# Attention kernel: the gates' matrix set up in the wait for the first keys, the last queries split behind the first maximum, the product's bank copied out by ScalarE

## The chip, the cores and the metric

The kernel runs on one core of a Trainium2 chip. The metric is the device time of one execution in microseconds (us). Engines are named as the profile names them: PE is TensorE's matmul row and PEld its weight load, DVE is VectorE, ACT is ScalarE, POOL is GpSimd, SP is SyncE, which issues nearly all DMAs.

## The reference

Three layers follow each other: attention with rotary positions, a mixture of experts with one expert per token, and a gated layer. The change touches the first one alone.

```
q_rot, k_rot = (rotate(q), rotate(k))          # 4 batches x 8 heads x 576 tokens x 64
scores = scale * q_rot @ k_rot^T
attn = exp(scores - max(scores))
attn = attn / (sum(attn) + 1e-9)
x = attn @ v                                   # tokens x 512
logits = x @ w_gate; expert = argmax(logits)   # 8 experts; a second gate w_output_gate
... experts, then  (sigmoid(x @ w_gate) * (x @ w_val)) @ w_out
```

## The kernel before

**Pairs and steps.** Two heads make a pair g, of which there are 16. A pair has 5 blocks of queries j: four of 128 queries of each head, and one (j = 4) that holds the last 64 queries of both. The text calls 5g + j the step t, from 0 to 79. The order of each engine's work is the order in which the code is written: the loop over t at lines 1042 to 1105 calls the pieces in turn, and every engine works through its own instructions in that order. In a step stand, one after the other:

- `scores(g, j)` (line 262): 12 matmuls (6 for j = 4) of queries and keys, each split in a rounded high part and a rest (`qTh`, `qTl`, `kTh`, `kTl`; `qDh`, `qDl` for the last 64 queries), into two PSUM tiles `s`; then DVE takes the two row maxima `nm` (L285) and ACT the two exponentials `p` (L292). There are two `s` tiles, so the scores of a step can only begin to overwrite them when the exponentials of the step before have read them.
- `pv` of step t - 2 (line 332): the product of weights and values, 18 matmuls (L339, L347) into the one PSUM bank `o` of the pair. After j = 1 and after j = 4 the bank's columns are copied into the SBUF tile `oT` (L349; L351 and L352).
- `turn_last` of step t - 1 (L310 on PE, copy L311 on DVE), then in some steps a piece of `xf`, which turns `oT` back to tokens with the matrix `wI` and divides by the sums, or of `tqk`, which turns the rotated queries and keys of the next pair (L241 and L249 on PE, halves on DVE by L230 and L231).
- `turn` of step t - 1: eight transposes of the weights in two PSUM tiles (L325), each copied by ACT into `pt` (L328). The PSUM tiles `t` come from a ring of three that `turn_last`, `tqk`, `xf` and `turn` share, so the second tile of `turn` needs the one that L311 reads.

POOL rotates the queries and keys two pairs ahead (`rot`, lines 188 to 212).

**The start.** Lines 977 to 995 load the first queries and keys, clear tiles on DVE and POOL, rotate pair 0 on DVE and turn it with `tqk(0, nc.scalar, (30, 8, 0))`: here ACT makes the high halves, and the numbers say how many transposes of the identity stand ahead of the keys, the queries and the tails (the last 64 of both). Their results are never read.

**Late set-up.** `late_setup` after step 2 clears `wI` on POOL and loads constants `mc` and the gates' columns of `wI`. `late_setup2` (line 1020) after step 5 fills `wI` with four identities, makes `tri`, `fold`, `ones`, `ids_tok` and `base` on DVE; `xf`, from step 8 on, and the routing of tokens to experts use them.

**Routing** of a batch (`route`, line 427) is spread over the steps 24 to 34, 44 to 54 and 64 to 74, mostly on DVE.

Of the kernel before, what the change touches and what calls it, by code (L numbers as in the profile page):

```python
# [9 lines left out]
F32 = mybir.dt.float32  # L10
# [5 lines left out]
ALU = mybir.AluOpType  # L16
# [27 lines left out]
XW = DM + 1  # L44
# [21 lines left out]
def tile_kernel(  # L66
# [144 lines left out]

        return a, b

    def tqk(g, eng=nc.vector, spin=(0, 0, 0)):

        i = g % 2

# [25 lines left out]

            return f

        def tails():
            ps = place(2)
            for n, nm in enumerate("kq"):
                nc.tensor.transpose(ps[:, 64 * n : 64 * n + 64], rotd.pop((g, nm))[0:64, 4, :], idf[0:64, 0:64])  # L249
            for c in (0, 576):  # L250
                halves_of(*(t[:, c : c + 64] for t in kT[i]), ps[:, 0:64], "k")
            for e in range(2):
                r = slice(64 * e, 64 * e + 64)
                halves_of(*(t[r, r] for t in qD[i]), ps[r, 64:128], "q")

        return [main("k"), main("q"), tails]

# [74 lines left out]
    def pv(g, j):  # L332
        if j == 0:
            OPS[g] = po.tile([128, 512], F32, tag="o", name="o")
        ps, src, (va, vd) = OPS[g], PT.pop((g, j)), vraw[g]
        q0, n = (128 * j, 128) if j < 4 else (0, 64)
        for c in range(4):
            for e in range(2):
                nc.tensor.matmul(  # L339
                    ps[64 * e : 64 * e + 64, q0 : q0 + n],  # L340
                    va[:, e, c, :],
                    src[:, 4 * e + c, :] if j < 4 else src[:, c, 64 * e : 64 * e + 64],
                    start=(c == 0),
                    stop=False,
                    skip_group_check=True,
                )
        nc.tensor.matmul(ps[:, q0 : q0 + n], vd, src[:, 8, 0:n], start=False, stop=True, skip_group_check=True)  # L347
        if j == 1:
            nc.vector.tensor_copy(O[g % 2][:, 0:256], ps[:, 0:256])  # L349
        elif j == 4:  # L350
            nc.vector.tensor_copy(O[g % 2][:, 256:512], ps[:, 256:512])  # L351
            nc.vector.tensor_copy(O[g % 2][:, 512:576], ps[:, 0:64])  # L352

# [628 lines left out]
        nc.vector.memset(t, 1.0)  # L984
    for t in (*(x.bitcast(F32) for x in (*qD[0], *qD[1])), *(vd for _, vd in vring + vlast)):
        nc.vector.memset(t, 0.0)
    load(1)
    load(0, "v")
    R = {nm: rot(0, nm) for nm in "kq"}
    for nm in "kq":  # L990
        for f in R[nm]:
            f(eng=nc.vector)
    first, gate_q = tqk(0, nc.scalar, (30, 8, 0)), rotd[0, "q"]
    for f in first:
        f()

    nc.gpsimd.tensor_copy(scr, gate_q[0:1, 0, 0:1])
    load(2)
# [4 lines left out]

    def late_setup():
        nc.sync.dma_start(out=mc, in_=misc)
        nc.gpsimd.memset(wI, 0.0)
        nc.gpsimd.memset(pinit, DUMMY)
        for t in O:
            nc.gpsimd.memset(t[:, 576:640], 0.0)
        nc.sync.dma_start(out=x_dram[0:1, :], in_=wI.rearrange("p h w -> p (h w)")[0:1, 0:XW])  # L1010
        for e in range(2):
            r = slice(64 * e, 64 * e + 64)
            for o, w in ((0, w_gate), (E, w_og)):
# [4 lines left out]
                )  # L1018

    def late_setup2():  # L1020
        nc.vector.tensor_copy(wI[:, :, 0:128], idf.unsqueeze(1).to_broadcast([128, 4, 128]))
        nc.vector.tensor_copy(tri, mc[:, 0:128])
        for o in range(2):
            nc.vector.tensor_tensor(
                out=fold[:, 64 * o : 64 * o + 64], in0=idf[:, 0:64], in1=idf[:, 64:128], op=ALU.add
            )
        nc.vector.memset(ones, 1.0)
        nc.vector.tensor_copy(ids_tok, mc[:, 128:148])
        nc.vector.tensor_copy(base, mc[:, 272:280])
        nc.sync.dma_start(out=perm_dram.rearrange("(p a) o -> p (a o)", p=128), in_=pinit)  # L1030

    M["seq"] = MAIN
# [9 lines left out]
    for t in range(NJ * NPAIR):  # L1042
        g, j = divmod(t, NJ)
        if t == NJ * (NPAIR - 1):
# [6 lines left out]
            gather(0)  # L1051
            gather(1)
        scores(g, j)
        if t >= 2:
            pv(*divmod(t - 2, NJ))
        if t >= 1:
# [316 lines left out]
```

## Time and profile before

| | us |
|---|---|
| median of 3 runs | 1128.62 |
| lowest, highest | 1127.61, 1129.76 |
| the profiled execution | 1129.55 |
| its span | 1127.8 |

The span goes from the first to the last instruction of the program in the profiled execution; 1.75 us lie around it. The attention fills the first 340 us or so of it. PE is the busiest engine, 95% of the span, DVE 68%, ACT 52%, POOL 32%. TensorE's clock has two levels, 2.4 GHz (1.00 in the profile) and 1.2 GHz (0.50); its mean share is 0.986.

### The profile page before, as it was taken

To read this page: it belongs to the slowest core of one execution; us is meant where nothing else is said; L and a number is where in the kernel's file an instruction comes from. 1 tells how busy PE (TensorE), PEld (TensorE's weight loads), DVE (VectorE), ACT (ScalarE), POOL (GpSimd) and SP (SyncE) were. 2 spreads that over 40 slices of the span, in tenths; PEclk is the share of its full clock that TensorE was granted. 3 is DMA by queue.
4 is the path that set the end of the run, shared out by engine and by line. 5 is a ranking of instruction groups with operands and counts; after the bars stand their busy time and mean duration, and the time that the engine had idled before them with its cause. 6 is when DMAs were issued, how large, how long until landed. Compare 5 with 4: busy or idle time off the path is not lost. (4 is left out here: it accounts for less than half of the span.)

```text
span 1127.8 us, 20456 instructions
## 1 busy us (share of the span) xinstructions
PE 1076.3 (95%) x7682; PEld 961.7 (85%) x7682; DVE 771.9 (68%) x1439; ACT 582.2 (52%) x1122; POOL 360.3 (32%) x336
## 2 busy tenths in 40 slices
PE   7799998989998999999999999999999999999998
PEld 6688787778777988988888889888999999999997
DVE  6778787787876886889989868854444545444442
ACT  4466455555544344667667656654444444444432
POOL 6335454553612103444333134521111111111111
PEclk8899999999999999999999999999999999999999
DMA  4144045045008297699999543300010010100000
GB/s 112 37 84 77 12 50 102 9 56 87 30 14 227 48 146 267 197 330 301 324 302 318 200 142 122 103 1 28 1 57 1 10 47 1 57 1 1 28 1 28
DMA packets 97053, 111.61 MB, mean 99 GB/s; under 512 B 16817, under 2 KB 75441, under 8 KB 96946
## 3 DMA queue, kind: packets, MB, share of 16 engines
q1 hardware_dynamic: 92482, 97.81, 31.2%
q0 software_dynamic: 4320, 12.08, 3.7%
q8 instruction: 62, 1.02, 0.4%
q14 instruction: 45, 0.37, 0.1%
q10 hardware_dynamic: 144, 0.33, 0.1%
HBM read 103.03 MB, written 15.56 MB: 105 GB/s over the span
## 5 line engine op out<-in xcount | busy, mean ns | idle before, releaser
L1242 POOL TENSOR_TENSOR gl<-gf,gh 128x384 fp32r<-128x384 f32 x72 | 73.3, 1018 | 348.6 <-ACT gh L1241 348.6
L292 ACT ACTIVATE p<-s,nm 128x576 f32<-128x576 f32 x144 | 105.6, 738 | 125.8 <-DVE nm L285 121.4
L771 DVE TENSOR_TENSOR lo<-wr,hi 128x1024 fp32r<-128x1024 f32 x112 | 156.4, 1409 | 14.7 <-ACT hi L770 14.3
L1237 DVE TENSOR_TENSOR gf<-v,sg 128x384 f32<-128x384 f32 x72 | 40.0, 555 | 134.0 <-PE v L1233 134.0
L285 DVE TENSOR_REDUCE nm<-s 128x1 f32<-128x576 f32 x144 | 102.9, 751 | 39.2 <-PE s L279 26.0
L1241 ACT CAST gh<-gf 128x384 fp32r<-128x384 f32 x72 | 36.9, 513 | 160.5 <-DVE gf L1237 160.5
L1216 DVE TENSOR_TENSOR gl<-gw,gh 128x512 fp32r<-128x512 f32 x72 | 72.9, 1012 | 66.8 <-ACT gh L1215 66.7
L770 ACT CAST hi<-wr 128x1024 fp32r<-128x1024 f32 x106 | 109.7, 1052 | 5.4 <-PE y L861 2.7
L325 PE MATMUL t<-idf,p 128*128 128x128 f32 x576 | 84.4, 282 | 19.0 <-DVE pt L311 16.7
L1231 PE MATMUL t<-yh,gh 128*128 128x384 f32 x288 | 99.1, 344 | 1.8 <-ACT gh L1215 1.6
L1233 PE MATMUL t<-yh,gl 128*128 128x384 f32 x288 | 97.4, 338 | 0.6 <-DVE gl L1216 0.2
L1232 PE MATMUL t<-yl,gh 128*128 128x384 f32 x288 | 96.7, 336 | 0.0
L1233 PE MATMUL v<-yh,vl 128*128 128x384 f32 x288 | 96.2, 334 | 0.0
L1231 PE MATMUL v<-yh,vh 128*128 128x384 f32 x288 | 96.2, 334 | 0.0
L1232 PE MATMUL v<-yl,vh 128*128 128x384 f32 x288 | 96.2, 334 | 0.0
L328 ACT COPY pt<-t 128x512 f32<-128x512 f32 x144 | 79.2, 589 | 31.3 <-PE t L325 30.7
L325 PEld LDWEIGHTS t<-idf,p 128*128 128x128 f32 x576 | 67.1, 146 | 27.1 <-DVE pt L311 21.3
L830 PE MATMUL h<-xl,hi 128*128 128x256 f32 x288 | 82.0, 285 | 1.8 <-DVE sc L806 1.8
L830 PE MATMUL h<-xh,hi 128*128 128x256 f32 x288 | 81.9, 284 | 0.7 <-DVE hl L835 0.7
L830 PE MATMUL h<-xh,lo 128*128 128x256 f32 x288 | 81.5, 283 | 0.0
L1235 ACT ACTIVATE sg<-t 128x384 f32<-128x384 f32 x72 | 35.3, 491 | 81.8 <-PE t L1233 81.8
L861 PE MATMUL y<-hi,hl 128*128 128x512 f32 x184 | 73.0, 397 | 4.6 <-DVE hl L847 4.4
(235 smaller groups left out, 2974.8 us busy)
## 6 DMA issues: line engine op xcount, KB each, us to landing
wr<-in_moe_w_dram SPq DMA_DIRECT2D x112, 512.0 KB
cv<-in_moe_w_gate_dram SPq DMA_DIRECT2D x12, 512.0 KB
cv<-in_moe_w_val_dram SPq DMA_DIRECT2D x12, 512.0 KB
cv<-in_moe_w_out_dram SPq DMA_DIRECT2D x12, 512.0 KB
yt<-y_dram SPq DMA_DIRECT2D x18, 256.0 KB
out_dram<-ob SPq DMA_DIRECT2D x18, 256.0 KB
kraw<-in_k_dram SPq DMA_DIRECT2D x16, 256.0 KB
qraw<-in_q_dram SPq DMA_DIRECT2D x16, 256.0 KB
```

Of the source, the lines that this page charges most:

```text
L285: nc.vector.tensor_reduce(out=nm, in_=s[:, :, 0:288], axis=AX.XY, op=ALU.max, negate=True)
L292: nc.scalar.activation(out=P[g, j][:, e, :].rearrange("p (a b) -> p a b", a=2), in_=s[:, :, 0:288], func=AF.Exp, bias=nm, scale=1.0, accum ...
L325: nc.tensor.transpose(ps[:, 128 * c : 128 * c + 128], src[:, e, k0 + 128 * c : k0 + 128 * c + 128], idf)
L328: nc.scalar.copy(dst[:, 4 * e : 4 * e + 4, :].rearrange("p c q -> p (c q)"), ps)
L770: nc.scalar.copy(out=hi, in_=t)
L771: nc.vector.tensor_tensor(out=lo, in0=t, in1=hi.bitcast(F32), op=ALU.subtract)
L830: nc.tensor.matmul(ps[:, c, :], w[:, kk, 128 * c : 128 * c + 128], x[:, kk, :], start=first, stop=last)
L861: nc.tensor.matmul(ps, hl, rh, start=False, stop=False)
L1231: nc.tensor.matmul(ps[:, 0:TG], wh[:, c], yh[:, kk, :], start=(kk == 0), stop=False)
L1232: nc.tensor.matmul(ps[:, 0:TG], wh[:, c], yl[:, kk, :], start=False, stop=False)
L1233: nc.tensor.matmul(ps[:, 0:TG], wl[:, c], yh[:, kk, :], start=False, stop=(kk == KD - 1))
L1242: nc.gpsimd.tensor_tensor(out=gl, in0=gf, in1=gh.bitcast(F32), op=ALU.subtract)
```

## The change

The memset of `wI`'s last columns, its four identities and `fold` now stand on DVE ahead of the rotation of pair 0. The tails of pair 0 are two pieces: the keys' is turned and halved between the keys and the queries, the queries' after the scores of step 0, behind 14 transposes of the identity; ahead of the queries stand 6 of these instead of 8. `tri`, `ids_tok` and `base` are copied by ACT after step 5, `ones` is set by POOL. The row of zeros in `x_dram` is written from `pinit` in 27 pieces instead of from `wI`. The three copies out of `o` are ACT's.

```diff
-    def tqk(g, eng=nc.vector, spin=(0, 0, 0)):
+    def tqk(g, eng=nc.vector, spin=(0, 0, 0, 0)):
...
-        def tails():
-            ps = place(2)
+        def tails(which="kq"):
+            ps = place(2 if "k" in which else 3)
             for n, nm in enumerate("kq"):
+                if nm not in which:
+                    continue
                 nc.tensor.transpose(ps[:, 64 * n : 64 * n + 64], rotd.pop((g, nm))[0:64, 4, :], idf[0:64, 0:64])
-            for c in (0, 576):
-                halves_of(*(t[:, c : c + 64] for t in kT[i]), ps[:, 0:64], "k")
-            for e in range(2):
-                r = slice(64 * e, 64 * e + 64)
-                halves_of(*(t[r, r] for t in qD[i]), ps[r, 64:128], "q")
+            if "k" in which:
+                for c in (0, 576):
+                    halves_of(*(t[:, c : c + 64] for t in kT[i]), ps[:, 0:64], "k")
+            if "q" in which:
+                for e in range(2):
+                    r = slice(64 * e, 64 * e + 64)
+                    halves_of(*(t[r, r] for t in qD[i]), ps[r, 64:128], "q")
...
         if j == 1:
-            nc.vector.tensor_copy(O[g % 2][:, 0:256], ps[:, 0:256])
+            nc.scalar.copy(O[g % 2][:, 0:256], ps[:, 0:256])
         elif j == 4:
-            nc.vector.tensor_copy(O[g % 2][:, 256:512], ps[:, 256:512])
-            nc.vector.tensor_copy(O[g % 2][:, 512:576], ps[:, 0:64])
+            nc.scalar.copy(O[g % 2][:, 256:512], ps[:, 256:512])
+            nc.scalar.copy(O[g % 2][:, 512:576], ps[:, 0:64])
...
+    nc.vector.memset(wI[:, :, 128:160], 0.0)
+    nc.vector.tensor_copy(wI[:, :, 0:128], idf.unsqueeze(1).to_broadcast([128, 4, 128]))
+    for o in range(2):
+        nc.vector.tensor_tensor(out=fold[:, 64 * o : 64 * o + 64], in0=idf[:, 0:64], in1=idf[:, 64:128], op=ALU.add)
     load(1)
     load(0, "v")
...
-    first, gate_q = tqk(0, nc.scalar, (30, 8, 0)), rotd[0, "q"]
-    for f in first:
-        f()
+    first, gate_q = tqk(0, nc.scalar, (30, 6, 0, 14)), rotd[0, "q"]
+    first[0]()
+    first[2]("k")
+    first[1]()
...
-        nc.gpsimd.memset(wI, 0.0)
...
-        nc.sync.dma_start(out=x_dram[0:1, :], in_=wI.rearrange("p h w -> p (h w)")[0:1, 0:XW])
+        nc.sync.dma_start(out=x_dram[0:1, :].rearrange("o (p c) -> (o p) c", p=27), in_=pinit[0:27, 0:19].bitcast(F32))
...
     def late_setup2():
-        nc.vector.tensor_copy(wI[:, :, 0:128], idf.unsqueeze(1).to_broadcast([128, 4, 128]))
-        nc.vector.tensor_copy(tri, mc[:, 0:128])
-        for o in range(2):
-            nc.vector.tensor_tensor(
-                out=fold[:, 64 * o : 64 * o + 64], in0=idf[:, 0:64], in1=idf[:, 64:128], op=ALU.add
-            )
-        nc.vector.memset(ones, 1.0)
-        nc.vector.tensor_copy(ids_tok, mc[:, 128:148])
-        nc.vector.tensor_copy(base, mc[:, 272:280])
+        nc.gpsimd.memset(ones, 1.0)
+        for o, c in ((tri, slice(0, 128)), (ids_tok, slice(128, 148)), (base, slice(272, 280))):
+            nc.scalar.copy(out=o, in_=mc[:, c])
...
         scores(g, j)
+        if t == 0:
+            first[2]("q")
```

What this does to the order of the engines is shown at three places. The numbers behind tile names tell buffers apart; `x2` stands for two in a row.

DVE at the start, from the rotation of pair 0's queries (`trq`) to the first maxima, before:

```order
L208 TENSOR_TENSOR trq<-ta,tb 128x2x5x64
L231 SCALAR_TENSOR_TENSOR kTl_150<-t,kTh_149 128x512
L231 SCALAR_TENSOR_TENSOR qTl_142<-t,qTh_141 128x512
L231 SCALAR_TENSOR_TENSOR kTl_150<-t,kTh_149 128x64 x2
L231 SCALAR_TENSOR_TENSOR qDl_146<-t,qDh_145 64x64 x2
L285 TENSOR_REDUCE nm<-s 128x1 x4
```

and now:

```order
L208 TENSOR_TENSOR trq<-ta,tb 128x2x5x64
L231 SCALAR_TENSOR_TENSOR kTl_150<-t,kTh_149 128x512
L231 SCALAR_TENSOR_TENSOR kTl_150<-t,kTh_149 128x64 x2
L231 SCALAR_TENSOR_TENSOR qTl_142<-t,qTh_141 128x512
L289 TENSOR_REDUCE nm<-s 128x1 x2
L231 SCALAR_TENSOR_TENSOR qDl_146<-t,qDh_145 64x64 x2
```

The keys' tails moved ahead of the queries, the queries' tails behind the first two maxima.

DVE from the first block of step 6 on, behind the keys of pair 2 (`kTl_150`), before:

```order
L231 SCALAR_TENSOR_TENSOR kTl_150<-t,kTh_149 128x512
L1021 COPY wI<-idf 128x4x128
L1022 CAST tri<-mc 128x128
L1024 TENSOR_TENSOR fold<-idf 128x64 x2
L1027 MEMSET ones 128x128
L1028 CAST ids_tok<-mc 128x20
L1029 COPY base<-mc 128x8
L285 TENSOR_REDUCE nm<-s 128x1 x2
L351 COPY oT_154<-o 128x256
L352 COPY oT_154<-o 128x64
L311 COPY pt<-t 128x128
```

and now:

```order
L231 SCALAR_TENSOR_TENSOR kTl_150<-t,kTh_149 128x512
L289 TENSOR_REDUCE nm<-s 128x1 x2
L315 COPY pt<-t 128x128
L230 TENSOR_SCALAR qTh_141<-t 128x512
L231 SCALAR_TENSOR_TENSOR qTl_142<-t,qTh_141 128x512
```

Between the keys and the maxima nothing is left, and none of the copies of `oT` ahead of L311 (now L315).

ACT at the same place, from the exponentials of step 5 to the copies `pt` of step 5, before:

```order
L292 ACTIVATE p,lsum_156<-s,nm 128x576 x2
L328 COPY pt<-t 128x512
L292 ACTIVATE p,lsum_156<-s,nm 128x576 x2
L328 COPY pt<-t 128x512 x2
L292 ACTIVATE p,lsum_156<-s,nm 128x576 x2
```

and now:

```order
L296 ACTIVATE p,lsum_156<-s,nm 128x576 x2
L332 COPY pt<-t 128x512
L1031 CAST tri<-mc 128x128
L1031 CAST ids_tok<-mc 128x20
L1031 COPY base<-mc 128x8
L296 ACTIVATE p,lsum_156<-s,nm 128x576 x2
L355 COPY oT_154<-o 128x256
L356 COPY oT_154<-o 128x64
L332 COPY pt<-t 128x512 x2
```

The three constants stand ahead of step 6's exponentials, the two copies of `oT` between these and the copies `pt`.

## Rows read from the trace of the kernel before

**Rows 1.** The page: busy time of the engines, share of the span, instructions.

```profile
PE 1076.3 (95%) x7682; PEld 961.7 (85%) x7682; DVE 771.9 (68%) x1439; ACT 582.2 (52%) x1122; POOL 360.3 (32%) x336
```

**Rows 2.** Timeline, steps 5 to 7: start, duration, engine, line, tiles, [idle before <-releaser].

```profile
36.51 1.48 DVE L1021 COPY wI<-idf 128x512 f32<-128x512 f32 x1
...
38.70 2.38 DVE L1024 TENSOR_TENSOR fold<-idf 128x64 f32<-128x64 f32 x2
...
41.83 1.41 DVE L285 TENSOR_REDUCE nm<-s 128x1 f32<-128x576 f32 x2
...
43.96 1.12 PE L325 MATMUL t<-idf,p 128*128 128x128 f32 x4 [5.92 <-DVE pt L311]
```

**Rows 3.** Windows: stretch, length, PE, PEld, DVE, ACT, POOL busy (instructions), PEclk, DMA, GB/s.

```profile
2.54:5.08 2.54, 2.54 (x13) 2.54 (x14) 0.01 (x1) 0.00 (x0) 0.00 (x0) 1.00 0.90 297
13.08:19.91 6.83, 4.45 (x23) 3.52 (x21) 3.37 (x7) 3.16 (x9) 6.67 (x7) 0.50 0.34 90
34.98:49.79 14.81, 8.89 (x86) 7.24 (x85) 12.62 (x25) 5.03 (x12) 9.47 (x8) 0.77 0.09 26
61.53:69.21 7.68, 7.47 (x86) 6.10 (x85) 6.92 (x17) 4.99 (x12) 2.24 (x2) 1.00 0.70 115
```

**Rows 4.** Timeline of DVE at the start.

```profile
5.08 0.82 DVE L193 TENSOR_TENSOR ta<-kraw,ropes 128x640 f32<-128x640 f32 x1 [2.54 <-DMA kraw<-in_k_dram]
```

**Rows 5.** Timeline of DVE at the start of the experts.

```profile
348.93 0.70 DVE L768 CAST hi<-wr 128x1024 fp32r<-128x1024 f32 x1 [2.47 <-DMA wr<-in_moe_w_dram]
```

**Rows 6.** Timeline, steps 0 and 1.

```profile
11.20 0.22 ACT L228 ACTIVATE kTh<-t 128x64 fp32r<-128x64 f32 x1
...
12.84 0.30 PE L279 MATMUL s<-kTl,qTh 64*128 64x288 f32 x2
...
13.72 1.42 DVE L285 TENSOR_REDUCE nm<-s 128x1 f32<-128x576 f32 x2
...
15.25 0.73 ACT L292 ACTIVATE p<-s,nm 128x576 f32<-128x576 f32 x1
...
15.40 1.32 PE L279 MATMUL s<-kTh,qTh 64*128 64x288 f32 x2 [2.27 <-ACT p L292]
...
17.73 1.42 DVE L285 TENSOR_REDUCE nm<-s 128x1 f32<-128x576 f32 x2 [2.58 <-PE s L279]
```

**Rows 7.** Windows of PE alone, in the identity's 30 transposes: busy (instructions), PEclk.

```profile
2.38:4.00 1.62, 1.62 (x8) 1.00 0.86 303
...
7.00:8.00 1.00, 1.00 (x10) 1.00 0.85 208
```

**Rows 8.** Timeline, step 16 (pair 3, block 1) and the start of step 17.

```profile
83.41 0.42 DVE L351 COPY oT<-o 128x256 f32<-128x256 f32 x1
...
83.65 0.73 ACT L292 ACTIVATE p<-s,nm 128x576 f32<-128x576 f32 x1
...
83.87 0.28 DVE L311 COPY pt<-t 128x128 f32<-128x128 f32 x1
...
84.20 0.42 PEld L325 LDWEIGHTS t<-idf,p 128*128 128x128 f32 x4 [0.44 <-DVE pt L311]
...
84.37 1.12 ACT L328 COPY pt<-t 128x512 f32<-128x512 f32 x2
84.79 0.19 PEld L279 LDWEIGHTS s<-kTh,qTh 64*128 64x128 f32 x2 [0.17 <-issue]
...
85.78 0.85 PEld L339 LDWEIGHTS o<-pt,v 128*64 128x64 f32 x16 [0.16 <-issue]
...
85.89 0.76 DVE L285 TENSOR_REDUCE nm<-s 128x1 f32<-128x576 f32 x1 [0.41 <-PE s L279]
```

**Rows 9.** Timeline, step 13 (block 3): ACT's copies of the weights.

```profile
73.17 1.07 ACT L328 COPY pt<-t 128x512 f32<-128x512 f32 x2 [0.46 <-PE t L325]
```

**Rows 10.** Loads of weights in routing, steps 26 and 27.

```profile
127.93 0.42 PEld L325 LDWEIGHTS t<-idf,p 128*128 128x128 f32 x4 [0.61 <-DVE pt L311]
```

**Rows 11.** Timeline, a long DVE instruction at step 54.

```profile
246.44 3.69 DVE L535 SCALAR_TENSOR_TENSOR den<-zs,den 128x5 f32<-128x5 f32 x1
```

## The prediction

> **What bounds the kernel now.** I read the page first: PE is busy 95% of the span, the others have room [rows 1]. So only what makes PE wait, or run at its lower clock, can be worth much, and I went through the attention step by step in the timeline for that. Three places concern this change. In step 6 PE stands 5.92 us for the copy L311, because DVE, which works in order, has the whole late set-up ahead of the maxima on which everything of that step hangs [rows 2]. At the start PE works through steps 0 and 1 with waits, and the granted clock is 0.50 (1.2 GHz) from 13.08 to 19.91 [rows 3, 6]. And in each pair's block 1 PE's weight loads wait 0.44 us for L311 behind the two copies of `oT` [rows 8]. Elsewhere the steps follow each other with PE full: the two steps 61.53 to 69.21 hold 7.47 us of PE work in 7.68 [rows 3].
>
> **Term 1, the late set-up leaves step 6.** From the scores of step 6 to those of step 8 pass 14.81 us; the same two steps one pair later, with the same 86 matmul records, take 7.68 [rows 3]. The difference, 7.13 us, is all that the set-up costs: DVE's block from 36.51 to 41.83, which is 5.32 us, and 1.8 us of work at the lower clock that followed the idle time (0.77 in the mean, against 1.00). What is late next is DVE's work on the keys of pair 2: it was free for the set-up at 36.51 [rows 2], 1.53 after the start of the scores at 34.98, while in step 17 the maxima start 85.89 - 84.79 = 1.10 after it [rows 8]. So 0.43 stays: a gain of 7.13 - 0.43 = 6.70 us.
>
> Where did the work go? ACT's three small copies, each between the 0.22 of 64 columns and half the 1.12 of two times 512 [rows 6, 8], come to between 0.7 and 1.7 us; at 128, 20 and 8 columns I take 0.7. They lie in front of step 6's exponentials, in the time in which ACT waits for the first maximum of the step, in every step; it has only the one copy `pt` of block 4 to do there. Without that cover they would delay the exponentials one for one. POOL's `ones` stands between rotations that are needed two pairs later, and POOL is rid of the memset of `wI`; nothing waits. SP's row of zeros waits for `pinit` instead of `wI`, both on POOL and in that order of lines; the loads behind it are used from step 8 on. All at nothing.
>
> **Term 2, the set-up in the wait for the first keys.** DVE is idle for 2.54 us up to the landing of the keys at 5.08 [rows 4]. Into it go a memset of 128 columns, a copy of 512 and two sums of 64. Their bounds: 1.48 + 2.38 us, as copy and sums took in step 5 beside a busy POOL [rows 2], which with the memset would end some 1.5 us after the keys and delay everything by that; or the row of a 1024-column cast on DVE, 0.70 [rows 5], for no more columns than all four have together (128 + 512 + 128 = 768), with some 0.1 for each further instruction about 1.0. POOL does nothing in this stretch, 0.00 [rows 3], so I take the lower value: hidden, with 1.5 us to spare.
>
> **Term 3, the split tails.** Before, the last scores of step 0 end at 13.14 but the maxima start only at 13.72, since the four tails in turn on ACT and DVE stand ahead [rows 6]. Now the keys' tails stand ahead of the queries' halves. ACT's second tail follows DVE's first, which is behind `kTl`; I expect it at 10.97, so that the queries' high half starts some 0.25 later than now, and the scores end at about 13.4 instead of 13.14. The maxima follow at once: 0.28 earlier than 13.72. The exponentials then end at 15.70 instead of 15.98. The queries' tails come behind them on ACT and are done on DVE by about 16.7, ahead of the next maxima: free as long as the scores of step 1 end later than that.
>
> The 14 transposes of the identity fill PE's 2.27 us of waiting [rows 6]. If they keep the clock up, the scores of step 1, which took from 15.40 to 17.92 at 1.2 GHz, take about 1.05 as in later steps and end at 16.85; their maxima, at 17.73 now, come 0.85 us earlier, and this carries through. But the clock fell at 13.08, before PE's long wait had begun, and the change takes activity away ahead of it, not adds any. If it falls all the same, the 14 take 0.20 us each, as the first 8 of the 30 did in 1.62 us, and not the 0.10 of the later ones [rows 7]: 2.9 us, to 16.6, which is later than the exponentials. Then the scores of step 1 end at 17.9 if the clock is back by then, no gain, or at 19.1 if it is not: 1.3 us lost. Between -0.85 and +1.3 I take 0.
>
> A rule speaks against these transposes. The Trainium skill, page "TensorE: Matmul & The Clock Gate", section "Part 4: PE-mode transpose", says that the full clock does not engage for transposes, as they do not count as PE activity in the same way. By that they would cost the 1.3 us and hold nothing. This trace disagrees in part: 30 transposes alone stood ahead when their pace went from 0.20 to 0.10 us each [rows 7].
>
> **Term 4, the copies out of the bank.** DVE is rid of three copies in each pair, ACT has them. In block 1 before, L311 started at 83.87 behind the two copies; now it starts where they did, at 83.41, and the 0.44 us wait goes. But the next wait stands right behind: the scores of step 17 need the second exponential, which ends at 83.65 + 0.73 = 84.38, so they start at 84.45 instead of 84.79, 0.34 earlier [rows 8]. And ACT now does both copies after that exponential: by the 0.22 of 64 columns and the 1.07 of two times 512 [rows 6, 9], some 0.37 and 0.22, less about 0.1 overlap each, 0.40. `pt` is then done at about 84.37 + 0.40 + 1.08 = 85.85 instead of 84.37 + 1.12 = 85.49, and the product that needs it starts at 85.92 instead of 85.78 [rows 8]. The gain of 0.34 becomes a loss of 0.14. In block 3 ACT waits 0.46 us for PE ahead of `pt` [rows 9], and the 256 columns fit in. Where routing makes DVE late, its shorter queue does help: the 0.61 us wait of step 27 [rows 10] shrinks by about 0.45; the three routings have some four such places, and about two where ACT has no slack in block 3 and 0.3 is lost. Sum: ten usual pairs at +0.14, four at -0.45, two at +0.3, that is +1.4 - 1.8 + 0.6 = +0.2. The bounds: -0.34 in 14 pairs, -4.8, and +0.3 in 14, +4.2, if ACT's copies cost 0.16 more than I think. I take 0.
>
> **Sum.** 6.70 us off the profiled execution's 1129.55 gives 1122.85; the median of the runs is 0.93 below that execution, so 1121.9.
>
> **The rivals.**
> - ScalarE keeps up, and block 1 gains its 0.34 in all 14 pairs: 1121.9 - 4.8 = 1117.1. For it: `pt` was done 0.29 ahead of the product [rows 8]. Against: the copies take more than that.
> - ACT's copies cost 0.3 in each pair: 1121.9 + 4.2 = 1126.1. For it: nothing but ACT's order decides; against: the two durations above.
> - The slower side: ScalarE becomes the bound of the attention. If each copy costs ACT the 0.42 that the wide one cost DVE [rows 8], without overlap, and a wait of its own besides, block 1 loses and block 3 eats its 0.46. The kernel is slower than before by more than 0.2% from 0.64 us a pair ((6.70 + 2.26) / 14); at 0.8 it is 1121.9 + 11.2 = 1133. Against: ACT's rows of 64 and 512 columns.
> - A pause goes or comes. DVE stood 3.69 us in one tiny instruction at step 54 [rows 11], and a second such pause stands in the trace; with the clock that falls after it, as after the 5.92 us in term 1 (1.8), each costs some 5 us. The change moves DVE's instructions against the loads. One gone: 1117; one more: 1127.
> - The 14 transposes hold nothing (the skill's rule above): 1121.9 + 1.3 = 1123.2.
> - The set-up isn't hidden at the start: 1121.9 + 1.5 = 1123.4, folded into the forecast's spread.
>
> **Chances.** Forecast, 1120 to 1124: 0.52. ScalarE keeps up: 0.15. Copies cost 0.3: 0.12. A pause gone 0.08, one more 0.05. Transposes hold nothing: 0.05. Slower: 0.03. A measurement of this kernel can tell 0.2%, 2.26 us, from no change, so faster means below 1126.36. That holds for the forecast, the first rival, a pause gone, the transposes, and rather more than half of the second: 0.87. Within 0.2%: the rest of it and one more pause, 0.10. Slower: 0.03. The range 1116.5 to 1126.0 leaves out one more pause, the slower side and part of the second rival, some 0.15.
>
> **What would show it.** Right: maxima of step 6 at about 36.6 of the new span, no wait over 0.5 us in steps 5 to 8 and clock 1.00 there; DVE's `fold` done ahead of the keys; L315's wait gone in block 1 and a new wait of PE for `pt` ahead of the product. Wrong: steps of pair 0 longer than 4.6 us, `fold` over 1 us each at the start, block 1 shorter than 3.8 us to the product, or DVE standing 3 us and more at other places.

## The result and the profile after

The changed kernel takes 1118.39 us, median of 4 runs (1117.05 to 1119.51), beside 1128.57 (1127.61 to 1129.76) of the kernel before on the same chip: 10.2 us less, a ratio of 0.990 (95% interval 0.9879 to 0.9921). A second set of 6 runs on another chip gave 1117.31 beside 1126.07: 0.9921 (0.9901 to 0.9940). The forecast was 1121.9 in 1116.5 to 1126.0: faster, as said, but by half as much again as the 6.7 us of the sum.

The profiled execution after took 1117.64 us, its span 1115.9 (before 1129.55 and 1127.8). The page's first part, beside [rows 1]: VectorE lost 18 us of busy time, ScalarE gained 10, TensorE has the same work in less time.

```profile
PE 1076.5 (96%) x7694; PEld 962.6 (86%) x7694; DVE 753.9 (68%) x1388; ACT 592.2 (53%) x1173; POOL 360.4 (32%) x336
```

Windows of after (stretch, length, busy time and instructions of PE, PEld, DVE, ACT, POOL, PEclk, DMA share, GB/s): from the first scores to those of step 5; the two steps from step 6 to step 8; the same two of the next pair.

```profile
11.88:30.80 18.92, 17.48 (x171) 14.53 (x171) 12.15 (x25) 10.91 (x28) 17.76 (x19) 1.00 0.20 46
34.31:42.08 7.77, 7.77 (x87) 6.46 (x86) 6.48 (x15) 5.72 (x17) 6.53 (x8) 1.00 0.18 50
53.81:61.57 7.76, 7.76 (x86) 6.45 (x86) 6.47 (x15) 5.32 (x14) 1.96 (x2) 1.00 0.70 116
```

The second row is the answer to the 14.81 us of [rows 3]: PE is busy all the time, at clock 1.00, and the steps are as long as the next pair's. The third shows that a usual pair gained nothing (7.76 now, 7.68 before).

**Where the time went**, stage by stage. Each number is the time between the first scores matmuls of two steps in the trace of one execution; the last column is the changed kernel on the second chip.

| steps | before | after | difference | after, again |
|---|---|---|---|---|
| start to 5 | 31.46 | 30.80 | -0.66 | 31.71 |
| 5 to 8 | 18.32 | 11.28 | -7.04 | 11.28 |
| 8 to 25 | 66.46 | 66.71 | +0.25 | 66.71 |
| 25 to 30 (first routing) | 22.96 | 21.93 | -1.03 | 21.93 |
| 30 to 64 | 147.03 | 146.26 | -0.8 | 144.9 |
| 64 to 79 (third routing, slots) | 66.98 | 64.16 | -2.8 | 64.31 |
| 79 to the end | 774.57 | 774.74 | +0.2 | 773.9 |

The differences add up to 11.9 us, by which these two executions differ; the medians differ by 10.2. Steps 5 to 30 agree in the two executions of the changed kernel to 0.1 us. Steps 30 to 64, the start and the end do not, to some 1 us. Within 30 to 64 lies the second routing: steps 45 to 50 took 23.00 us before, 22.18 and 21.97 after.

### The profile page after: what moved, and what is told of

The parts are those of the page before. It is cut to its first block, busy times and chain, and to the rows that moved or that the text cites. A ratio compares the mean times of both kernels' runs of the same rounds, so it can differ in the third digit from the quotient of the medians.

```text
span 1115.9 us, 20490 instructions
## 1 busy us (share of the span) xinstructions
PE 1076.5 (96%) x7694; PEld 962.6 (86%) x7694; DVE 753.9 (68%) x1388; ACT 592.2 (53%) x1173; POOL 360.4 (32%) x336
## 5 line engine op out<-in xcount | busy, mean ns | idle before, releaser
L775 DVE TENSOR_TENSOR lo<-wr,hi 128x1024 fp32r<-128x1024 f32 x112 | 156.2, 1408 | 14.9 <-ACT hi L774 14.6
L1220 DVE TENSOR_TENSOR gl<-gw,gh 128x512 fp32r<-128x512 f32 x72 | 72.9, 1012 | 66.9 <-ACT gh L1219 66.8
L329 PE MATMUL t<-idf,p 128*128 128x128 f32 x576 | 81.3, 280 | 6.0 <-DVE pt L315 3.7
L1260 PE MATMUL o<-oh,gl 128*128 128x512 f32 x192 | 76.3, 397 | 0.1
```

The costliest lines, as they stand in the source:

```text
L329: nc.tensor.transpose(ps[:, 128 * c : 128 * c + 128], src[:, e, k0 + 128 * c : k0 + 128 * c + 128], idf)
L775: nc.vector.tensor_tensor(out=lo, in0=t, in1=hi.bitcast(F32), op=ALU.subtract)
L1260: nc.tensor.matmul(ps, gl[:, c], wh, start=False, stop=(f == NF - 1))
```

## The experiments

Fourteen traces (before, after and one of each run below) carry what follows; every time was taken beside the kernel before on the same chip, so kernels of different chips are compared by their ratio to it. A single median here has an interval of some 2 us to either side. Up to step 30 the traces of kernels whose code in a stretch is the same agree to 0.2 us, so differences of stretches decide where medians can't. Later stretches spread more: steps 64 to 79 took 66.98, 65.14 and 65.46 us in before and experiments 2 and 3, whose code there is the same.

### 1. The late set-up back in step 5

```diff
-    nc.vector.memset(wI[:, :, 128:160], 0.0)
-    nc.vector.tensor_copy(wI[:, :, 0:128], idf.unsqueeze(1).to_broadcast([128, 4, 128]))
-    for o in range(2):
...
     def late_setup2():
-        nc.gpsimd.memset(ones, 1.0)
...
-            nc.scalar.copy(out=o, in_=mc[:, c])
+        nc.vector.tensor_copy(wI[:, :, 0:128], idf.unsqueeze(1).to_broadcast([128, 4, 128]))
+        nc.vector.tensor_copy(tri, mc[:, 0:128])
+        for o in range(2):
...
+        nc.vector.tensor_copy(base, mc[:, 272:280])
```

> The changed kernel with the late set-up alone back as it was: on VectorE behind the maxima of step 5, the memset of wI on GpSimd; start, split tails and copies out of the bank as changed. Theory (the set-up cost 7.1 us of waiting in steps 5 to 7 and nothing at the start): 6.7 to 7.1 us above the changed kernel, about 1125.3, with the wait of step 6 back and the times of steps 0 to 4 unchanged to 0.1 us. Rival (most of what was won came from elsewhere, the set-up at the start costs something too): under 5 us above the changed kernel, and steps 0 to 4 earlier by 0.2 us or more.

Measured: 1119.89, ratio 0.9937 (0.9914 to 0.9959), 2 to 4 us above the changed kernel by the ratios. Steps 5 to 10 take 22.94 us beside 19.50: only 3.44 more. That is between the 6.7 to 7.1 of the theory and nothing, and steps 0 to 4 came no earlier, though the rival wanted that. The same instructions, in the same place, were done in 2.3 us, where they had taken 5.3. VectorE and GpSimd in that stretch (start, duration, engine, line, operation, tiles, [idle before <-releaser]):

```profile
36.45 0.42 DVE L1026 COPY wI<-idf 128x512 f32<-128x512 f32 x1
36.79 0.22 DVE L1027 CAST tri<-mc 128x128 bf16<-128x128 f32 x1
36.92 0.36 DVE L1029 TENSOR_TENSOR fold<-idf 128x64 f32<-128x64 f32 x2
37.25 0.17 DVE L1032 MEMSET ones<- 128x128 bf16 x1
37.33 1.43 DVE L1033 CAST ids_tok<-mc 128x20 int32<-128x20 f32 x1
...
38.75 1.41 DVE L289 TENSOR_REDUCE nm<-s 128x1 f32<-128x576 f32 x2
```

```profile
37.19 1.54 POOL L193 TENSOR_TENSOR ta<-kraw,ropes 128x640 f32<-128x640 f32 x1 [6.89 <-DMA kraw<-in_k_dram]
38.69 1.67 POOL L200 TENSOR_TENSOR tb<-kraw,ropes 128x320 f32<-128x320 f32 x2
```

The copy of `wI` took 0.42 here and 1.48 in [rows 2], the two sums of `fold` 0.36 against 2.38. GpSimd was still idle. The first instruction with an input that met it, a cast of 20 columns issued at 37.33, ended at 38.76, 0.03 after GpSimd's L193. In the kernel before, GpSimd had begun a little earlier:

```profile
36.16 1.55 POOL L193 TENSOR_TENSOR ta<-kraw,ropes 128x640 f32<-128x640 f32 x1 [6.20 <-DMA kraw<-in_k_dram]
37.66 1.85 POOL L200 TENSOR_TENSOR tb<-kraw,ropes 128x320 f32<-128x320 f32 x2
39.47 1.53 POOL L193 TENSOR_TENSOR ta<-qraw,ropes 128x640 f32<-128x640 f32 x1
```

There the copy of `wI` ended at 37.99, 0.28 after the first L193, and the two sums of `fold` at 39.59 and 41.08, each 0.08 after a GpSimd instruction (39.51 and 41.00).

New theory: VectorE's instructions on tiles in SBUF stand until GpSimd's running one has ended, and this, not their work, was most of what the set-up cost.

### 2. The kernel before, its set-up one step earlier

```diff
-        if t == 5:
+        if t == 4:
             late_setup2()
```

> The kernel before, with its late set-up on VectorE called one step earlier, behind the tails of step 4, where GpSimd does nothing; nothing else is changed. Theory (VectorE's instructions on tiles in SBUF stand still until GpSimd's running instruction ends, so the set-up took 5.32 us beside GpSimd's rotation and would take 1.4 to 1.6 without it): step 5's maxima 1.2 to 1.6 us later, steps 6 and 7 back to about 3.5 and 4, the kernel 4.5 to 5.5 us faster than before, about 1121.5. Rival (the set-up's own work and its place on VectorE cost the 7 us): the wait of some 5 us is then found in step 5, the kernel within 1 us of before.

Measured: 1120.04, ratio 0.9946 (0.9926 to 0.9966), 6.0 us faster than before by this one number. VectorE has the same instructions, now with GpSimd idle until 37.26:

```profile
33.12 0.43 DVE L1021 COPY wI<-idf 128x512 f32<-128x512 f32 x1
33.46 0.22 DVE L1022 CAST tri<-mc 128x128 bf16<-128x128 f32 x1
33.60 0.35 DVE L1024 TENSOR_TENSOR fold<-idf 128x64 f32<-128x64 f32 x2
33.93 0.17 DVE L1027 MEMSET ones<- 128x128 bf16 x1
34.01 0.11 DVE L1028 CAST ids_tok<-mc 128x20 int32<-128x20 f32 x1
34.03 0.15 DVE L1029 COPY base<-mc 128x8 f32<-128x8 f32 x1
34.22 1.42 DVE L285 TENSOR_REDUCE nm<-s 128x1 f32<-128x576 f32 x2
```

1.06 us in place of 5.32. Steps 4 to 8 take 15.75 us (22.13 before): 6.4 us of the 7 are had without moving the set-up off VectorE's path at all. The theory holds.

### 3. The kernel before with the move of the set-up alone

Against the kernel before, and with the row of zeros taken from `pinit`, as changed:

```diff
+    nc.vector.memset(wI[:, :, 128:160], 0.0)
+    nc.vector.tensor_copy(wI[:, :, 0:128], idf.unsqueeze(1).to_broadcast([128, 4, 128]))
+    for o in range(2):
...
     def late_setup2():
-        nc.vector.tensor_copy(wI[:, :, 0:128], idf.unsqueeze(1).to_broadcast([128, 4, 128]))
...
+        nc.gpsimd.memset(ones, 1.0)
...
+            nc.scalar.copy(out=o, in_=mc[:, c])
```

> The kernel before with the move of the set-up alone (early on VectorE, three copies on ScalarE, ones on GpSimd); start, tails and copies out of the bank as before. Theory: 6.7 to 7.1 us faster than before, about 1119.5 to 1121, all of it in steps 5 to 7; usual pairs 19.4, routing steps as before. Rival (the parts help each other: the late maxima of step 6 cost so much only because VectorE met GpSimd there): 3 to 4 us faster.

Measured: 1120.48, ratio 0.9955 (0.9929 to 0.9981). Steps 5 to 8 take 11.19 us, 7.13 less than before; and the ratio's interval, 2 to 8 us of 1126, holds both that and the 5.6 of the medians. In the stretch itself the rival's 3 to 4 us are out. Steps 25 to 30 stay at 23.0. Steps 64 to 79 took 65.46, 1.5 less than before; experiment 4, with the same move and VectorE's copies too, has 66.80, so that difference is the spread of these steps and not the move.

### 4. The three copies back on VectorE

```diff
-            nc.scalar.copy(O[g % 2][:, 0:256], ps[:, 0:256])
+            nc.vector.tensor_copy(O[g % 2][:, 0:256], ps[:, 0:256])
...
-            nc.scalar.copy(O[g % 2][:, 256:512], ps[:, 256:512])
-            nc.scalar.copy(O[g % 2][:, 512:576], ps[:, 0:64])
+            nc.vector.tensor_copy(O[g % 2][:, 256:512], ps[:, 256:512])
+            nc.vector.tensor_copy(O[g % 2][:, 512:576], ps[:, 0:64])
```

> The changed kernel with the three copies of oT back on VectorE. Theory (the copies bring about 0.4 to 0.5 us at each of the routing steps that wait for a ring tile behind VectorE, and more in the third routing and the work on slots, and cost 0.1 in a usual pair): 2.5 to 4 us above the changed kernel, with steps 27, 29 and 65 to 75 longer by what they had lost, and the usual pairs' steps shorter by 0.1 us a pair. Rival (as predicted, the copies come to nothing and the rest is chance in where pauses fall): within 1 us of the changed kernel.

Measured: 1121.52 (12 runs), ratio 0.9955 (0.9936 to 0.9974), 4 to 6 us above the changed kernel by the ratios. Usual pairs 19.40 (19.49 as changed), steps 25 to 30 23.11 (21.93), 64 to 79 66.8 (64.2). So the copies are worth 1.2 us in the first routing and cost 0.1 in a usual pair, as the theory said. In steps 64 to 79 they are worth 2.6 by this trace, and 1 to 3 by the four traces that have them on VectorE (before, experiments 2, 3 and 4: 65.1 to 67.0). The waits of the weight loads of the transposes for VectorE's copy L315, from 38 to 340 us of the span (total us, times, longest), first with the copies back, then as changed:

```profile
PEld t L329 <- DVE pt L315: 11.6, 15, 2.0
```

```profile
PEld t L329 <- DVE pt L315: 3.9, 6, 1.6
```

### 5. Block 1's copy on ScalarE, block 4's on VectorE

```diff
         elif j == 4:
-            nc.scalar.copy(O[g % 2][:, 256:512], ps[:, 256:512])
-            nc.scalar.copy(O[g % 2][:, 512:576], ps[:, 0:64])
+            nc.vector.tensor_copy(O[g % 2][:, 256:512], ps[:, 256:512])
+            nc.vector.tensor_copy(O[g % 2][:, 512:576], ps[:, 0:64])
```

> The changed kernel with block 4's two copies on VectorE where they were, ahead of the copy pt; block 1's copy stays on ScalarE. Tells which copies cost the usual pairs 0.1 us and which bring the gain of the routing steps. Theory (block 4's copies trade a wait for L315 against one for ScalarE's pt, block 1's are free): usual pairs 19.40, step 26 again 4.3, steps 28 and 70 to 75 as in the changed kernel, 5.09 and 21.6. Rival (block 1's copy costs or brings nothing): all steps as with the three copies back, 5.62 in step 28 and 22.55 in 70 to 75.

Measured: 1120.28, ratio 0.9930 (0.9917 to 0.9943). Usual pairs 19.40, step 26 4.31 (3.86 as changed), step 28 5.29 (5.09 as changed, 5.62 with all copies back). So block 4's copies cost the 0.1 in usual pairs and bring the 0.45 in step 26; block 1's bring 0.33 of step 28, the rest is block 4's. Steps 70 to 75 took 24.09, where the theory had 21.6 and the rival 22.55; neither explains that.

### 6. Block 4's copies on VectorE behind L315

```diff
         elif j == 4:
-            nc.scalar.copy(O[g % 2][:, 256:512], ps[:, 256:512])
-            nc.scalar.copy(O[g % 2][:, 512:576], ps[:, 0:64])
+            def out():
+                nc.vector.tensor_copy(O[g % 2][:, 256:512], ps[:, 256:512])
+                nc.vector.tensor_copy(O[g % 2][:, 512:576], ps[:, 0:64])
...
+                late.append(out)
...
             turn_last(*divmod(t - 1, NJ))
+        while late:
+            late.pop()()
```

> The changed kernel with the two copies of block 4 on VectorE again, but behind the copy pt on which the next weight loads wait; block 1's copy stays on ScalarE. Theory (the weight loads of block 1 wait for ScalarE's pt or for the copy L315, whichever has the oT copies ahead of it; behind both they cost nothing): the usual pairs' five steps 19.0 to 19.15 us in place of 19.49, 3 to 4 us faster than the changed kernel over ten pairs, less up to 0.5 in each routing. Rival (the next wait stands right behind, at the transposed block or the exponentials): 19.3 to 19.5, within 1 us of the changed kernel.

Measured: usual pairs 19.13, 0.36 below the changed kernel and 0.27 below before, as the theory said. But 1118.13, ratio 0.9929 (0.9911 to 0.9947), is no gain: steps 25 to 30 take 22.65 (21.93), 30 to 35 20.61 (19.84 and 19.96). Probably the copies are in the way of what stands behind them in VectorE's late steps; which wait it is was not read. From step 5 to 79 it was still faster (308.03 us; 310.33 and 309.12 as changed), and lost that behind step 79 (776.5; 774.7 and 773.9), for a reason that isn't known.

### 7. Behind L315 in usual pairs, on ScalarE where routing follows

Against experiment 6:

```diff
+            cp = nc.scalar.copy if g in (4, 5, 8, 9, 12, 13, 15) else nc.vector.tensor_copy
...
-                nc.vector.tensor_copy(O[g % 2][:, 256:512], ps[:, 256:512])
-                nc.vector.tensor_copy(O[g % 2][:, 512:576], ps[:, 0:64])
+                cp(O[g % 2][:, 256:512], ps[:, 256:512])
+                cp(O[g % 2][:, 512:576], ps[:, 0:64])
...
-            if g < NPAIR - 1:
-                late.append(out)
+            if g in (4, 5, 8, 9, 12, 13, 15):
+                out()
```

> The changed kernel with block 4's copies of oT on VectorE behind the copy pt in the nine pairs 0 to 3, 6, 7, 10, 11 and 14, and on ScalarE as changed in the others, whose products end in routing steps. Theory (0.36 us a usual pair, nothing given back in the routing): usual five steps 19.13, steps 25 to 35 as in the changed kernel (21.9 and 19.9), 3 us faster than the changed kernel, a ratio to before of about 0.989. Rival (the gain is lost again in steps whose pauses shift with VectorE's place): a ratio of 0.992 or more.

Measured: 1118.80, ratio 0.9914 (0.9885 to 0.9943). The stretches came out: usual pairs 19.14, steps 25 to 35 41.8. The time didn't: 1 to 3 us each were lost in steps 35 to 40 (26.35), 50 to 55 (21.47) and 70 to 75 (24.32). A gain over the changed kernel can't be told from none.

### 8. The start as before

```diff
-    first, gate_q = tqk(0, nc.scalar, (30, 6, 0, 14)), rotd[0, "q"]
-    first[0]()
-    first[2]("k")
-    first[1]()
+    first, gate_q = tqk(0, nc.scalar, (30, 8, 0, 0)), rotd[0, "q"]
+    for f in first:
+        f()
...
-        if t == 0:
-            first[2]("q")
```

> The changed kernel with the start of pair 0 alone as it was: 30 and 8 identity transposes, the queries' tails ahead of the first maximum, no 14 transposes. Theory (the split and the held clock brought the 0.8 us seen at the scores of step 4): 0.8 us above the changed kernel, the granted clock at 0.50 from about 13 to 20 us, maxima of step 1 at about 17.7 in place of 16.9. Rival (the new set-up ahead of the keys is what keeps the clock or the starts early): no difference, maxima of step 1 stay at 16.9 to 17.1.

Measured: 1118.01, ratio 0.9924 (0.9901 to 0.9947), not told apart from the changed kernel. From the first scores to those of step 5 pass 20.76 us (18.92 and 20.04 as changed), the granted clock 0.50 (1.2 GHz) from about 14.6 to 21.

### 9. Without the 14 transposes, and the changed kernel again

```diff
-    first, gate_q = tqk(0, nc.scalar, (30, 6, 0, 14)), rotd[0, "q"]
+    first, gate_q = tqk(0, nc.scalar, (30, 6, 0, 0)), rotd[0, "q"]
```

> The changed kernel without the 14 identity transposes ahead of the scores of step 1; everything else as changed. Theory (they hold the clock): the granted clock falls to 0.50 behind the scores of step 0, the scores of step 1 take 2.5 us in place of 1.8, maxima of step 1 at about 17.7 in place of 16.9, the kernel 0.8 us longer. Rival (by the Trainium skill, page TensorE: Matmul & The Clock Gate, Part 4: transposes don't engage the full clock, so they hold nothing): clock 1.00 and maxima at 16.9 without them too, no difference in the time.

> The changed kernel itself once more, as the measure for the others on the same chip and for the start: with the 14 identity transposes the granted clock stayed at 1.00 behind the scores of step 0 in two profiles and fell to 0.50 in one (with the set-up back). Theory (they hold it in some executions alone): either may come; the time 1116 to 1120, and the slots and steps behind the second pair as in the first profile to 0.3 us. Rival (they hold it always, and the set-up put back was what let it fall): clock 1.00 up to step 5 again, maxima of step 1 at about 16.9.

Measured: 1119.41 without them, ratio 0.9926 (0.9904 to 0.9948); the time doesn't tell them apart. The traces do. Windows of the changed kernel, its first execution and the second, over the 14 transposes (1.00 is 2.4 GHz, 0.50 is 1.2):

```profile
13.47:15.22 1.75, 1.75 (x17) 1.58 (x15) 1.42 (x2) 0.87 (x3) 1.67 (x2) 1.00 0.75 192
```

```profile
13.26:16.51 3.25, 3.25 (x18) 2.92 (x17) 1.42 (x2) 1.55 (x4) 3.17 (x3) 0.50 0.60 158
17.00:18.00 1.00, 1.00 (x14) 0.84 (x12) 0.60 (x3) 0.27 (x2) 1.00 (x2) 1.00 0.00 0
```

And without them, over the scores of step 1:

```profile
14.92:17.45 2.53, 2.41 (x13) 1.81 (x14) 0.64 (x3) 0.99 (x4) 2.53 (x4) 0.50 0.31 77
```

Nine traces have the 14 transposes. In three (after, experiments 4 and 7) the clock stayed at 1.00 and the stretch from the first scores to those of step 5 took 18.8 to 18.9 us; in six it fell as the transposes began or in the scores ahead of them, they took up to 3.25 us in place of 1.75, and the stretch took 19.8 to 20.1. Five traces lack them (before, experiments 2, 3, 8, 9): the clock fell in all, and the stretch took 20.1 to 20.9. So the transposes don't always hold the clock, but where it falls all the same it is back earlier (1.00 from 17 on, where experiment 9's scores still ran at 0.50 to 17.45). Of the five, experiment 9 alone has the split tails, so it is the one to compare with: its stretch took 20.5 us, which is also the mean of the five, and by it the transposes are worth 1.6 us where the clock holds (18.9 in the mean) and 0.5 where it falls (20.0).

### 10. The last gate operations of routing one step later

The pauses of [rows 11] look like the set-up. In after, at the end of step 34, VectorE and GpSimd:

```profile
150.94 0.16 DVE L535 TENSOR_SCALAR den<-den 128x5 f32<-128x5 f32 x1
151.20 3.62 DVE L539 SCALAR_TENSOR_TENSOR den<-zs,den 128x5 f32<-128x5 f32 x1
154.85 0.19 DVE L546 RECIPROCAL x<-den 128x5 f32<-128x5 f32 x1
```

```profile
150.82 0.90 POOL L513 DMA_INDIRECT perm_dram<-ids_tok,pi  x1 [0.23 <-issue]
151.74 1.55 POOL L208 TENSOR_TENSOR trk<-ta,tb 128x640 f32<-128x640 f32 x1
153.24 1.54 POOL L208 TENSOR_TENSOR trq<-ta,tb 128x640 f32<-128x640 f32 x1
```

An operation on 5 columns ends at 154.82, GpSimd's second L208 at 154.78. In before, [rows 11] end at 250.13, and there GpSimd's last L208 ended at 250.10:

```profile
248.56 1.54 POOL L208 TENSOR_TENSOR trq<-ta,tb 128x640 f32<-128x640 f32 x1
```

So these operations were moved to where GpSimd has nothing to do:

```diff
             [gate_sum],
+            *([[]] if b < B - 2 else []),
             [guard, both, weight],
```

> The changed kernel with the three last gate operations of the first and second routing (guard, both, weight: tiny instructions of VectorE on tiles in SBUF) called one step later, when GpSimd has done its two L208 of the coming pair; the third routing as it was. Theory (the two pauses of 3.6 us are VectorE standing until GpSimd's L208 end, as the set-up stood in step 6): no VectorE instruction of 3 us in steps 34 and 54, steps 35 to 40 and 55 to 60 at 19.5 to 20.5 us in place of 23.9, the kernel 7 to 9 us faster than the changed one, about 1109. Rival (the pause has another cause, such as loading of instructions, and happens at that time whatever stands there): another instruction stands 3.6 us, no gain over 1 us.

Measured: 1120.32, ratio 0.9933 (0.9920 to 0.9946): no gain. The three operations take 0.16 to 0.19 us each now, so GpSimd was what they stood for. But VectorE and ScalarE stop all the same in that place, in step 54, for a release that the trace doesn't show:

```profile
239.88 0.29 DVE L315 COPY pt<-t 128x128 f32<-128x128 f32 x1 [3.59 <-remote]
```

```profile
240.76 1.08 ACT L332 COPY pt<-t 128x512 f32<-128x512 f32 x2 [3.54 <-remote]
```

Behind that stop another VectorE instruction met GpSimd's two L208 (from 239.45 to 242.49) and ended 0.04 after them:

```profile
240.84 1.69 DVE L396 TENSOR_SCALAR r<-lsum 128x4 f32<-128x4 f32 x1
```

In the traces of experiments 7 and 11 such an operation on `lsum` (there L405) stood 3.26 and 3.23 us in step 35. Steps 35 to 40 took 24.88 (25.22 and 23.88 as changed), 55 to 60 21.51 (23.84 and 23.89), 50 to 55 22.02 (19.90 and 20.49), and 70 to 75, whose code is the same, 26.55 (21.6). What stops the engines for 3 to 4 us in these steps, and shows up elsewhere when VectorE's order is changed, stays open; it was not the gate operations' wait for GpSimd alone. The rival's loading of instructions isn't seen in the stop of step 54: from 236.3 to 239.8 the DMA rows hold no packet of an instruction queue. GpSimd was issuing its indirect DMAs in these microseconds, until 239.4.

### 11. Both: gate operations later and copies behind

```diff
+            *([[]] if b < B - 2 else []),
...
+            cp = nc.scalar.copy if g in (4, 5, 12, 13, 15) else nc.vector.tensor_copy
...
+            if g in (4, 5, 12, 13, 15):
+                out()
+            else:
+                late.append(out)
...
+        while late:
+            late.pop()()
```

> The same as the kernel with the later gate operations, and block 4's copies of oT on VectorE behind the copy pt in the ten pairs without routing behind them (in pairs 4, 5, 12, 13 and 15 they stay on ScalarE). Theory: another 0.36 us in each of some nine pairs, 3 us: about 1106, usual pairs 19.13, steps 25 to 35 as in the changed kernel. Rival (the gain in the usual pairs moves VectorE against GpSimd so that other instructions stand): within 1 us of the kernel with the later gate operations alone.

Measured: 1120.23, ratio 0.9924 (0.9910 to 0.9938). Usual pairs 19.13, but 70 to 75 27.17 and 50 to 55 22.61: as in experiment 10, and no better than the changed kernel.

## Why the prediction came out as it did

**What bounds.** Right: only the places in which PE stood were worth anything.

**Term 1, -6.70 forecast, -7.04 measured** (-7.13 in experiment 3). The price of the stretch was read rightly from two windows. Two steps in it were not. The 0.43 us that were to stay did not:

```profile
33.62 0.46 DVE L321 COPY pt<-t 64x64 f32<-64x64 f32 x2 [0.32 <-ACT p L296]
...
34.84 0.69 DVE L231 SCALAR_TENSOR_TENSOR kTl<-t,kTh 128x512 fp32r<-128x512 f32 x1
35.45 1.41 DVE L289 TENSOR_REDUCE nm<-s 128x1 f32<-128x576 f32 x2
```

The maxima of step 6 in after start 0.04 behind the end of its scores (35.41), right behind `kTl`; VectorE got there 1.14 after the start of the scores (34.31), as in later steps, not 1.53. The 1.53 were read from a step 5 in which VectorE had stood longer ahead of the same copy (L317 before, L321 now):

```profile
34.69 0.46 DVE L317 COPY pt<-t 64x64 f32<-64x64 f32 x2 [0.72 <-PE t L241]
```

Why it stood 0.72 us there and 0.32 now isn't shown. ScalarE's three small copies took 0.70 us together (0.30, 0.21, 0.19), as estimated, and ScalarE still waited 0.82 us for the maxima behind them. And the cause was named too simply as the set-up's work: 1.06 us of the 5.32 were work, the rest stood for GpSimd. The prediction had it ("beside a busy POOL"), but as a bound for the new place, not as a second way to win the same time.

**Term 2, taken 0: right.** The new set-up at the start:

```profile
2.51 0.17 DVE L991 MEMSET wI<- 128x128 f32 x1
2.59 0.36 DVE L992 COPY wI<-idf 128x512 f32<-128x512 f32 x1
2.87 0.34 DVE L994 TENSOR_TENSOR fold<-idf 128x64 f32<-128x64 f32 x2
5.46 0.83 DVE L193 TENSOR_TENSOR ta<-kraw,ropes 128x640 f32<-128x640 f32 x1 [2.25 <-DMA kraw<-in_k_dram]
```

Some 0.7 us (1.0 was estimated), and VectorE still waits 2.25 us for the keys. The choice of the lower bound because POOL is idle there was the decisive one, and experiments 1 and 2 show why.

**Term 3, taken 0 between -0.85 and +1.3: a small gain.** In the first execution the clock held and step 5 came 0.66 earlier; from the first scores it is 1.2 less than before (the keys landed 0.38 us later in this execution). In the second it fell, and the same stretch took 20.04 against 20.10. The +1.3 was never seen: where the clock falls the transposes are as slow as feared (3.25 us), but behind them it is back, so the scores of step 1 don't run slowly as well. The rule that was weighed, the Trainium skill's in "TensorE: Matmul & The Clock Gate", section "Part 4: PE-mode transpose", that transposes don't engage the full clock, fits neither outcome: in after the transposes ran at 1.00 to their end and the clock didn't fall behind them, where without them (experiment 9) it fell at 14.9; and in the second execution, where it fell as they began, it was back at 16.7, while in experiment 9 it stayed at 0.50 until 21.7. These are single executions.

**Term 4, taken 0: this is the step that failed.** The usual pair was right in kind and nearly in size: +0.08 to +0.10 measured, +0.14 forecast. Step 16 and the start of step 17 in after, beside [rows 8]:

```profile
75.76 0.28 DVE L315 COPY pt<-t 128x128 f32<-128x128 f32 x1
...
76.72 0.37 ACT L355 COPY oT<-o 128x256 f32<-128x256 f32 x1
...
76.98 0.23 ACT L356 COPY oT<-o 128x64 f32<-128x64 f32 x1
77.08 1.10 ACT L332 COPY pt<-t 128x512 f32<-128x512 f32 x2
...
77.87 0.19 PEld L343 LDWEIGHTS o<-pt,v 128*64 128x64 f32 x2 [0.16 <-ACT pt L332]
...
78.23 0.85 PEld L343 LDWEIGHTS o<-pt,v 128*64 128x64 f32 x14 [0.17 <-ACT pt L332]
```

The wait for L315 is gone, the copies cost 0.37 and 0.23 as worked out, and the product waits for `pt` in its place. What failed is the count of places outside the usual pairs: four at -0.45 and two at +0.3, -1.2 in all. The first routing alone gave -1.03. Of it -0.46 came in step 26, the size that was forecast, but at another wait, which the prediction didn't name, this one of before:

```profile
123.51 0.42 PEld L325 LDWEIGHTS t<-idf,p 128*128 128x128 f32 x4 [0.92 <-DVE pt L311]
```

It is 0.46 in after. The wait of [rows 10] is gone, but its step 27 is only 0.04 shorter: there, as in a usual pair, the product waits for `pt` in its place. Another -0.53 came in step 28; the second routing gave -0.8 and -1.0 in the two executions, and the third with the slots -2.8, 1 to 3 of it the copies' (experiment 4). Step 28's chain wasn't seen. With the copies back (experiment 4) it reads:

```profile
123.14 0.42 DVE L353 COPY oT<-o 128x256 f32<-128x256 f32 x1
...
124.40 0.55 DVE L406 TENSOR_TENSOR x<-t,r 128x384 f32<-128x384 f32 x1
```

```profile
124.56 1.07 ACT L332 COPY pt<-t 128x512 f32<-128x512 f32 x2 [0.36 <-PE t L329]
```

```profile
125.19 0.17 PE L484 MATMUL t<-ohb,tri 128*128 128x8 bf16 x1 [0.29 <-ACT pt L332]
```

and in after:

```profile
124.79 0.10 PEld L484 LDWEIGHTS <-tri 128*128 128x128 bf16 x1 [0.18 <-DVE x L406]
```

L484 are small matmuls of the routing, into a tile of the ring `t`. As changed, and in experiments 5 and 6, they start 0.05 us behind the end of L406 on VectorE. With block 1's copy on VectorE (before, experiments 3 and 4) L406 ends earlier than they start by 0.24, and they start 0.05 behind the end of the first of ScalarE's two copies `pt` (125.14 here). So the copy moves two things: VectorE's queue down to L406, which ends 4.55 us after the scores of step 28 in experiment 4, 4.39 in experiment 5 and 4.20 as changed, and the release that L484 wait for. Why that changes, perhaps the ring's tile that they are given, isn't shown. Block 1's copy cost nothing in block 3: usual pairs are 19.40 with it on either engine (experiments 4 and 5). In all the copies brought 3 to 6 us: from step 5 to 79 pass 309.1 to 310.3 us with them on ScalarE (after, twice, and experiments 8 and 9), 313.4 and 314.8 with them on VectorE (experiments 3 and 4). Of this +0.9 lies in ten usual pairs, the rest in routing and slots, where the sum had +1.4 and -1.2.

**Rivals.** ScalarE kept up, but not in the way of the first rival: the gain lies in the routing, not in block 1 of the usual pairs. ScalarE as a bound, and copies at 0.3 a pair, are out. Pauses come and go between executions and kernels, as the fourth rival said, and hide differences of 2 us. The measured 1118.4 lies below the 1120 to 1124 that the forecast gave itself and inside the range, whose lower end stood there for the first rival and for a pause gone; the gain that reached it came from neither, so that the range held is in part luck.

## What to carry to other kernels

When an instruction takes several times its usual duration, look at what GpSimd did in the same microseconds before pricing its work: one step to where GpSimd is idle gave here nearly all that taking the work away gave. A copy moved to another engine isn't worth the wait that it removes in the regular steps, where the next wait stands close behind, but what it frees in the steps in which its old engine is late; count those from the waits of each such step. And an engine's order in front of a wait can be worth more than the choice of engine: the same copies behind the one instruction that TensorE waits for beat both kernels in the usual pairs (19.13 us beside 19.40 and 19.49), though no gain in the kernel's time could be told.

## What the runs showed of the hardware

- **VectorE stands for GpSimd.** A VectorE copy, cast or two-input operation on tiles in SBUF, met by a running GpSimd tensor operation, ended behind it. Small ones ended 0.03 to 0.04 us after it: 1.43 us for a cast of 20 columns (0.11 alone), 3.62 for 5 columns (0.17 alone); the copy of 512 columns ended 0.28 after. The maxima, which read PSUM, took 1.41 to 1.42 beside GpSimd as without it, and the memset of `ones` 0.17 in both. The Trainium skill, "SBUF — State Buffer", section "Who interferes with whom", has it as one pair of ports that the two engines lock for a whole instruction; the traces agree.
- **Whether VectorE gets in between two GpSimd instructions differs.** The 3.62 us lasted through two L208 in a row. In step 6 of before VectorE got in each time: the two sums of `fold` ended 0.08 behind two GpSimd instructions that followed each other. What decides it isn't shown.
- **The clock at the start isn't the same in each execution of the same program**: 1.00 throughout in one, 0.50 from about 13.3 to 16.7 us in the other.
